# Earlier request of the block inverses and another queue for late stores, in an RWKV-7 attention fused with a squared-ReLU feed-forward

## The chip, the cores and the metric

One core of a Trainium2 chip runs the whole program. The metric is the device time of one execution in microseconds (us). Four executions of the kernel before took 956.38, 958.85, 961.85 and 968.67 us, a median of 960.35 us. The execution that was profiled took 956.67 us, of which the profile's span covers 954.7 us; the rest, 1.97 us, lies around the span.

## What is computed

For each of 4 batches and 8 heads, a 40 x 40 state is carried over 768 time steps, with `y_t = r_t S`, and then `S <- S * w_t - (S a_t) b_t^T + v_t k_t^T`:

```python
for t in range(S):
    y[:, :, t] = np.einsum('bhd,bhde->bhe', rt, state)
    Sa = np.einsum('bhde,bhe->bhd', state, at)
    state_decay = state * wt[:, :, None, :] - np.einsum('bhd,bhe->bhde', Sa, bt)
    state = state_decay + np.einsum('bhd,bhe->bhde', vt, kt)
...
h = np.maximum(x @ w_in, 0.0)          # x: 3072 tokens x 320, w_in: 320 x 2048
return (h * h @ w_out).astype(np.float32)
```

All is float32, the two weights of the second part are float64 in memory.

## The kernel before

**Chunks.** The sequence is cut into 24 chunks of 128 steps (6 along time, 4 batches; chunk i is batch i % 4). Within a chunk the recurrence is solved as a triangular system. For chunk i, `early(i)` (line 360) transposes w, a and b, forms the running products of the decays on VectorE, and multiplies out the triangular matrix N, which ScalarE copies out of PSUM with six copies (lines 398 to 402). N is then stored to DRAM: for chunks from 14 on (`SMALL`), four transfers into `kept_d` and one into `kept_n`. The decays go to `kept_e`.

**Inverses.** GpSimd inverts N's blocks. Chunks are taken in units: chunks 2 to 13 in pairs, then 14 to 17, 18 to 21, and 22 and 23. `take` (line 442) loads a unit's blocks from `kept_q` or `kept_d` into `half_n`, `solving` (line 456) runs the substitution with two tensor operations a step, and stores the result to `kept_t`. For a chunk below 14 only 32 x 32 blocks are inverted, and `inverses(i)` (line 495) puts the 64 x 64 inverse T together. It is a generator of four stages, one taken at each `join()`: (1) request the transfers `blocks` (two, line 508), `N` (line 489) and `spares` (two, line 493); (2) VectorE transposes `blocks` (line 515), ScalarE spreads them into T (line 517); (3) TensorE multiplies (line 525), ScalarE copies (527); (4) TensorE multiplies again (532), ScalarE copies the rest of T (534). `blocks` has one buffer. For a chunk from 14 on, stage 1 loads T as a whole (line 502) and nothing else is left to do.

**Slots.** The first 7 chunks are laid out by hand in a list of steps. Then, for i from 7 to 23, `sorted_slot(i)` (line 973) is one round of some 31 to 38 us: the chain of chunk i (`ch`), everything that chunk j = i + 1 needs (`turn_rv`, `make_rv`, `turn_k`, `turn_down`, `scale_kb`, `make_a`, its `join`s), `early` of one or two chunks ahead (`one`, `two`), and a share of the feed-forward (`thirds`, `whole`, `square`, `make_quarter`). Slot 7 prepares chunks 14 and 15, slot 8 chunks 16 and 17, slots 9 to 14 one chunk each, 18 to 23. Every engine runs its instructions in the order in which this text issues them. `store` and `later` put a transfer off by one or two steps.

**Where the joins stand.** `early_join` is true where chunk j is the second of its pair: stage 1 was then already requested at the end of the slot before, in `loads` (line 956). Where j is the first of a pair (below 14: j = 10 in slot 9 and j = 12 in slot 11) stage 1 comes at line 999, after the slot's fifth step, stage 2 at 1006, stage 3 at 1011 and stage 4 at the end of the slot.

**Queues.** Nearly all transfers are issued by SyncE (SP). Each transfer that SyncE or ScalarE issues takes the next of eight completion semaphores, shared by the two, in turn, and the built program makes it wait until the transfer that had this semaphore before has landed. An engine that issues a transfer stands still during such a wait.

**Buffers that matter here.** `ps_c` and `ps_f` are PSUM pools of two banks each. `turn_state` puts a transposed state into a `ps_c` bank that ScalarE empties into `sd` (line 595); the next chain's first product (`x_`, line 633) needs that bank. `whole` fills both `ps_f` banks, which ScalarE empties into `hid` (line 757).

Of the kernel before, what the change touches and what calls it, by code (L numbers as in the profile page):

```python
# [17 lines left out]
def kernel(  # L18
# [22 lines left out]
    nc = tc.nc  # L41
# [6 lines left out]
    HC = C // 2  # L48
# [11 lines left out]
    at = 0  # L60
    for h, d, n in ((6, 0, D), (7, 0, D), (5, HALF, D - HALF)):
        while n:
# [5 lines left out]
            d, n = d + m_, n - m_  # L68
# [23 lines left out]
    def new(name, shape, bufs):  # L92
        return work.tile(shape, FP32, tag=name, name=name, bufs=bufs)
# [7 lines left out]
    def tick():  # L101
        for entry in line:
            entry[0] -= 1
        while line and line[0][0] <= 0:
            line.pop(0)[1]()
# [3 lines left out]
    def store(out_, in_, steps=2, queue=nc.sync):  # L109
        later(lambda: queue.dma_start(out=out_, in_=in_), steps)  # L110
# [198 lines left out]
    kept_n = [dram.tile([HC, H, HC], FP32, tag=f"n{i}", name=f"kept_n{i}") for i in range(len(order))]  # L309
    Q = HC // 2  # L310
# [17 lines left out]
    def turn(x_):  # L328
        p_ = psum(ps_w)
        for q in range(NP):  # L330
            nc.tensor.transpose(p_[:, q * 128:(q + 1) * 128], pair(x_, q), ident)  # L331
        return quads(p_)

    def products(l_, r_):

        ps = [quads(psum(ps_w)) for _ in range(2)]
        for q in range(NP):
            for e in range(2):
                rows = slice(e * DP, e * DP + D)
                mm(ps[e][:, q], l_[rows, q, :], r_[rows, q, :], True)  # L340
        return ps
# [18 lines left out]
    def early(i, g=None, apart=False):  # L360

        x_ = early_loaded.pop(i)
        dec = decays.next() if g is None else kept_here[i]
        opened = i in opened_early
        if g is not None:
            g["dec"] = dec
            nc.vector.memset(dec[:, :A_, :, MID:MID + 1], 1.0)
        up, down, aT = (dec[:, n] for n in (UP, DOWN, A_))
        wT = turn(x_["w"])
        yield  # L370
        for q in range(NP):
            nc.vector.tensor_tensor_scan(up[:, q, MID + 1:C + 1], wT[:, q, MID:], ones, 1.0, Alu.mult, Alu.mult)  # L372
            nc.vector.tensor_tensor_scan(down[:, q, MID - 1::-1], wT[:, q, MID - 1::-1], ones, 1.0, Alu.mult, Alu.mult)
        yield
        if not apart:
            bT_, aT_ = turn(x_["b"]), turn(x_["a"])
        nc.vector.reciprocal(up[:, :, 0], down[:, :, 0])
        nc.vector.reciprocal(down[:, :, C], up[:, :, C])
        for q in range(NP):
            nc.vector.tensor_tensor_scan(up[:, q, 1:MID], wT[:, q, :MID - 1], ones[:, 1:], up[:, q, 0:1], Alu.mult, Alu.mult)  # L380
            nc.vector.tensor_tensor_scan(down[:, q, C - 1:MID:-1], wT[:, q, C - 1:MID:-1], ones[:, 1:], down[:, q, C:C + 1], Alu.mult, Alu.mult)  # L381
        yield
        if apart:
            bT_, aT_ = turn(x_["b"]), turn(x_["a"])
            yield
        bT = turned("bT", 1)
        nc.vector.tensor_tensor(bT, bT_, down[:, :, 1:C + 1], Alu.mult)
        nc.vector.tensor_tensor(aT[:, :, :C], aT_, up[:, :, :C], Alu.mult)  # L388
        if opened:
            waiting["e", i] = lambda: on_queue[0].dma_start(out=kept_e[i], in_=dec[:USED])  # L390
        else:
            store(kept_e[i], dec[:USED], 2)
        yield
        bb, c = order[i]
        t_ = new("N", [128, 2, H, HC], 1)
        for e, p_ in enumerate(products(bT, aT[:, :, :C])):
            plain, flip_ = t_[:, :, e:NP:2], t_[:, :, NP + e::2]
            nc.scalar.copy(plain, p_[:, ::2].rearrange("s h (f t) -> s f h t", f=2))  # L398
            for half in range(2):
                own_, other = (slice(n * HC, (n + 1) * HC) for n in (half, 1 - half))  # L400
                nc.scalar.copy(flip_[own_, half], p_[other, 1::2, other])
            nc.scalar.copy(flip_[:HC, 1], p_[:HC, 1::2, HC:])
        moved = []
        joins = lambda half, f=Q: t_[half * HC:half * HC + Q, half, :, f:]
        for half in range(2):
            for n in range(2):
                at = half * HC + n * Q
                if i < SMALL:
                    kept, to = kept_q[i, :, half, n], at + Q
                else:  # L410
                    u = unit_of[i]
                    kept, to = kept_d[u][i - units[u][0], :, half], (half + 1) * HC
                    kept = kept[:, n * Q * HC:n * Q * HC + Q * (to - at)].rearrange("h (s t) -> h s t", s=Q)
                moved.append((kept.rearrange("h s t -> s h t"), t_[at:at + Q, half, :, n * Q:to - half * HC], nc.scalar if g is not None and n else nc.sync))
            if i < SMALL and g is None:
                moved.append((kept_m[i][half], joins(half, 0), nc.sync))
        if g is None:
            moved.append((kept_n[i], t_[:HC, 1], nc.sync))
        if opened:
            waiting["n", i] = lambda: [(queue if queue is nc.scalar else on_queue[0]).dma_start(out=to, in_=in_) for to, in_, queue in moved]  # L420
        else:
            for to, in_, queue in moved:
                store(to, in_, 1, queue)
        if g is not None:
            g["N"] = new("N21", [HC, H, HC], 2)
            nc.scalar.copy(g["N"], t_[:HC, 1])
            g["joins"] = spare("joins", i)
            for half in range(2):
                nc.scalar.copy(g["joins"][half * HC:half * HC + Q], joins(half))
        yield  # L430
# [166 lines left out]
    def begin(i, g):  # L597
        g["x"] = loaded.pop(i)
        g["up"], g["aT"] = g["dec"][:, UP], g["dec"][:, A_, :, :C]
# [206 lines left out]
    def run(gen):  # L806
        for _ in gen:
            tick()
# [13 lines left out]
    def prepare(i, g=None, apart=False, steps=0):  # L822
        gen = early(i, g, apart)
        for _ in range(steps):
            next(gen)
            yield
        if i + 1 < len(order) and i + 1 not in early_loaded:
            load_early(i + 1)
        yield from gen
# [97 lines left out]
    for word in """  # L927
# [5 lines left out]
        at = word[len(kind):]  # L933
# [32 lines left out]
    def step(*what):  # L966
        for w_ in what:
            w_()
        tick()
# [3 lines left out]
    def sorted_slot(i, g, ch):  # L973
        j = i + 1
        more = j < len(order)
        n = ready.setdefault(j, {}) if more else None
        made = [prepare(m_, apart=True) for m_ in ahead.get(i, ())]
        one, two = (made + [iter(()), iter(())])[:2]
        if j in inversions:
            n["joining"] = inversions.pop(j)  # L980
        early_join = more and "joining" in n
        joining = n.pop("joining") if early_join else inverses(j, n) if more else iter(())
        fine = more and unit_of[j] < FINE
        join = on(joining)
        of = lambda fn: (lambda: fn(j, n)) if more else (lambda: None)

        if more and "x" in n:
            n.update(up=n["dec"][:, UP], aT=n["dec"][:, A_, :, :C])
        elif more:
            begin(j, n)  # L990
        step(second.make_quarter)
        step(of(turn_rv), on(one), on(one))
        fetch_next(j + 1, "r")
        step(second.make_quarter)
        step(on(ch), of(decay_state))
        step(of(make_rv), second.thirds)
        step(on(ch), on(one))
        if fine:
            join()
        step(second.whole)  # L1000
        step(on(ch))
        step(on(one), of(turn_k))
        step(on(one), on(ch), of(turn_down))
        step(on(ch), of(scale_kb))
        if fine:
            join()
        step(on(ch), of(make_a), second.thirds, on(one))
        fetch_next(j + 1, "v")
        step(of(turn_state), second.square, second.whole, on(two))
        if not early_join:  # L1010
            join()
        run(ch)
        if more:
            begin_chain(j, n)
        loads(j + 1)
        step(second.square, second.make_quarter, on(two), on(two))
        if i in ahead and len(ahead[i]) > 1:
            step(on(two), on(two))
        step(second.make_quarter, on(two))
        for gen in (one, two, joining):  # L1020
            run(gen)

    for i in range(LAID, len(order)):
        tc.no_sync_barrier()
        g = ready.pop(i)
# [41 lines left out]
```

## Time and profile before

| | |
|---|---|
| profiled execution | 956.67 us, span 954.7 us |
| four executions | 956.38 to 968.67 us, median 960.35 us |
| TensorE, matmuls | 903.6 us busy, 95% of the span |
| VectorE / ScalarE / GpSimd | 452.2 / 286.8 / 530.2 us busy |
| mean granted TensorE clock | 0.971 |
| moved by DMA | 103.36 MB, mean 108 GB/s |
| packets of SyncE's queue (q1) and ScalarE's (q10) | 246869 and 2650 |

The page shares the span out by engine, and its chain of waits follows the work that ended last back from the last instruction. The timeline lists one engine's instructions in order of time, merged where they repeat: start, time, engine and line, operation, out<-in, shapes, and in brackets how long the engine stood idle before and who ended it. In SyncE's rows (SPq) the time is that of issuing, and it holds the time for which the queue could take no more. When a transfer lands is read from the trace's completion events. TensorE had these gaps of more than 0.12 us after 300 us of the span: 0.48 us at 364.85, 0.45 us at 402.08, 3.91 us at 423.90, 0.40 us at 870.06.

### The profile page before, as it was taken

To read this page: it belongs to the slowest core of one execution; us is meant where nothing else is said; L and a number is where in the kernel's file an instruction comes from. 1 tells how busy PE (TensorE), PEld (TensorE's weight loads), DVE (VectorE), ACT (ScalarE), POOL (GpSimd) and SP (SyncE) were. 2 spreads that over 40 slices of the span, in tenths; PEclk is the share of its full clock that TensorE was granted. 3 is DMA by queue.
4 is the path that set the end of the run, shared out by engine and by line. 5 is a ranking of instruction groups with operands and counts; after the bars stand their busy time and mean duration, and the time that the engine had idled before them with its cause. 6 is when DMAs were issued, how large, how long until landed. Compare 5 with 4: busy or idle time off the path is not lost.

```text
span 954.7 us, 22650 instructions
## 1 busy us (share of the span) xinstructions
PE 903.6 (95%) x9156; PEld 717.8 (75%) x9156; DVE 452.2 (47%) x1064; ACT 286.8 (30%) x735; POOL 530.2 (56%) x1001
## 2 busy tenths in 40 slices
PE   5878989779999999989999999999999999999998
PEld 4545656558787887878888888888888878887776
DVE  4526738787863455543654554543334432231110
ACT  3223244444533233323333332222212222222111
POOL 4788518265018678139999849999768850000000
PEclk9989979799999999999999999999999999999999
DMA  9689777785875587994554786605664154120000
GB/s 110 127 153 178 151 138 150 165 184 119 165 134 129 110 174 127 168 177 81 115 91 83 131 171 113 113 19 82 137 110 75 35 108 79 39 35 9 13 14 14
DMA packets 253223, 103.36 MB, mean 108 GB/s; under 512 B 234144, under 2 KB 240160, under 8 KB 251968
## 3 DMA queue, kind: packets, MB, share of 16 engines
q1 hardware_dynamic: 246869, 83.43, 48.5%
q0 software_dynamic: 3600, 16.25, 7.2%
q10 hardware_dynamic: 2650, 2.25, 0.8%
q8 instruction: 72, 1.18, 0.6%
q14 instruction: 32, 0.25, 0.1%
HBM read 69.00 MB, written 30.92 MB: 105 GB/s over the span
## 4 chain that ended last, share of the span: by engine, by line
PE 72%; DVE 4%; DMA 3%; ACT 1%; SPq 1%; issue 1%; ACTq 0%; DVEq 0%
PE ps_f L87 40%; PE ps_w L87 13%; PE ps_c L87 12%; PE ps_w L331 4%; PE ps_c L593 1%; DMA hid<-in_moe_w_out_dram 1%; PE ps_c L666 1%; DMA dec<-kept_e 1%; PE ps_w L577 1%; DMA blocks<-kept_t 1%; SPq L508 1%; DVE decay L381 0%; DVE decay L380 0%; DVE decay L388 0%; DVE hid L764 0%
## 5 line engine op out<-in xcount | busy, mean ns | idle before, releaser
L477 POOL TENSOR_TENSOR half_p<-half_n,half_t 128x126 f32<-128x126 f32 (+44 forms) x437 | 231.9, 531 | 75.6 <-DMA half_n<-kept_d 22.4
L479 POOL TENSOR_TENSOR half_t<-half_t,half_p 128x126 f32<-128x126 f32 (+44 forms) x437 | 248.2, 568 | 34.3
L87 PE MATMUL ps_f<-w_out,hid 128*128 128x320 f32 x768 | 218.7, 436 | 0.0
L87 PEld LDWEIGHTS ps_f<-w_out,hid 128*128 128x128 f32 x768 | 142.0, 190 | 54.0 <-issue 0.2
L87 PE MATMUL ps_f<-tokens,w_in 128*128 128x256 f32 x672 | 157.8, 389 | 0.0
L87 PEld LDWEIGHTS ps_f<-tokens,w_in 128*128 128x128 f32 x672 | 126.9, 194 | 18.7 <-issue 1.7
L764 DVE TENSOR_TENSOR hid<-hid 128x512 f32<-128x512 f32 x96 | 81.0, 882 | 50.1 <-ACT hid L757 49.7
L757 ACT ACTIVATE hid<-ps_f 128x512 f32<-128x512 f32 x84 | 49.9, 597 | 84.1 <-PE ps_f L87 84.1
L264 PE MATMUL ps_f<-ident 128*128 128x512 f32 (+2 forms) x148 | 70.6, 615 | 0.0
L451 POOL DMA_DIRECT2D half_n<-kept_q x18 | 9.4, 528 | 78.0 <-DMA kept_q<-N 31.1
L692 DVE TENSOR_TENSOR tokens<-ps_c,dec 128x512 f32<-128x512 f32 x24 | 16.6, 690 | 76.2 <-PE ps_c L87 76.2
L347 DVE TENSOR_TENSOR RV<-ps_w,upper 128x512 f32<-128x512 f32 x48 | 30.9, 686 | 45.7 <-PE ps_w L87 45.4
L372 DVE TENSOR_TENSOR_SCAN decay<-ps_w,ones 128x64 f32<-128x64 f32 x88 | 23.9, 271 | 60.0 <-PE ps_w L331 59.9
L264 PEld LDWEIGHTS ps_f<-ident 128*128 128x128 f32 x148 | 29.0, 213 | 26.6 <-issue 25.5
L87 PE MATMUL ps_f<-tokens,w_third 64*128 64x256 f32 x336 | 45.5, 380 | 3.3 <-ACT hid L757 3.3
L347 DVE TENSOR_TENSOR RX<-ps_w,upper 128x512 f32<-128x512 f32 x48 | 30.8, 684 | 37.2 <-PE ps_w L87 36.9
L543 DVE TENSOR_TENSOR kvT<-ps_w,dec 128x512 f32<-128x512 f32 x24 | 16.5, 687 | 62.0 <-ACT minus_x L653 35.2
L87 PEld LDWEIGHTS ps_c<-xr,T 64*64 64x64 f32 x768 | 28.0, 139 | 19.6 <-issue 16.3
L398 ACT COPY N<-ps_w 128x256 f32<-128x256 f32 x48 | 17.7, 368 | 80.7 <-PE ps_w L87 54.6
L565 DVE TENSOR_TENSOR f<-end,dec 128x4 f32<-128x4 f32 x20 | 5.4, 271 | 67.9 <-DMA dec<-kept_e 67.9
L555 ACT COPY rT<-ps_w 128x512 f32<-128x512 f32 x24 | 14.0, 584 | 77.6 <-PE ps_w L331 77.5
L87 PE MATMUL ps_w<-decay,bT 40*128 40x128 f32 x352 | 28.2, 294 | 7.7 <-DVE RX L347 3.9
(146 smaller groups left out, 1432.7 us busy)
## 6 DMA issues: line engine op xcount, KB each, us to landing
dec<-kept_e SPq DMA_DIRECT2D x22, 633.8 KB
kept_e<-decay SPq DMA_DIRECT2D x19, 633.8 KB
in_w<-in_w_dram SPq DMA_DIRECT2D x24, 160.0 KB
in_b<-in_b_dram SPq DMA_DIRECT2D x24, 160.0 KB
in_ab<-in_a_dram SPq DMA_DIRECT2D x24, 160.0 KB
in_r<-in_r_dram SPq DMA_DIRECT2D x24, 160.0 KB
in_v<-in_v_dram SPq DMA_DIRECT2D x24, 160.0 KB
out_dram<-o SPq DMA_DIRECT2D x24, 160.0 KB
```

The costliest lines, as they stand in the source:

```text
L87: nc.tensor.matmul(o, l_, r_, start=start, stop=True, skip_group_check=True)
L264: nc.tensor.matmul(fill_bank[:, :n * 128], ident, ident.unsqueeze(1).to_broadcast([128, n, 128]), start=True, stop=True, skip_group_check= ...
L331: nc.tensor.transpose(p_[:, q * 128:(q + 1) * 128], pair(x_, q), ident)
L347: nc.vector.tensor_tensor(t_, p_, over4(upper), Alu.mult)
L372: nc.vector.tensor_tensor_scan(up[:, q, MID + 1:C + 1], wT[:, q, MID:], ones, 1.0, Alu.mult, Alu.mult)
L398: nc.scalar.copy(plain, p_[:, ::2].rearrange("s h (f t) -> s f h t", f=2))
L477: nc.gpsimd.tensor_tensor(p_, part[:, at:at + m_].unsqueeze(1).to_broadcast([128, n, m_]), t3[:, :n, s:s + 1].to_broadcast([128, n, m_]), ...
L479: nc.gpsimd.tensor_tensor(t3[:, :n, s + 1:], t3[:, :n, s + 1:], p_, Alu.subtract)
L543: nc.vector.tensor_tensor(kT, kT_, down[:, :, 1:C + 1], Alu.mult)
L692: nc.vector.tensor_tensor(t_, y_, g["up"][:, :, :C], Alu.mult)
L757: nc.scalar.activation(h_, p_.rearrange("p f t -> p (f t)"), Act.Relu)
L764: nc.vector.tensor_tensor(h_, h_, h_, Alu.mult)
```

## The change

Two edits. Stores of N (`kept_d` and `kept_n`) of chunks that are not in the hand-laid opening, that is from 14 on, are issued by ScalarE instead of SyncE: five transfers for each of ten chunks. And stage 1 of `inverses` for the first chunk of a pair is taken right after the slot's first `make_quarter` instead of at line 999, so that each of its later stages moves one join ahead (stage 2 to line 999, stage 3 to 1006); the join at line 1011 is left out for these slots.

```diff
@@ early
-                moved.append((kept..., t_[...], nc.scalar if g is not None and n else nc.sync))
+                moved.append((kept..., t_[...], nc.scalar if not opened or g is not None and n else nc.sync))
...
-            moved.append((kept_n[i], t_[:HC, 1], nc.sync))
+            moved.append((kept_n[i], t_[:HC, 1], nc.sync if opened else nc.scalar))
@@ sorted_slot
         step(second.make_quarter)
+        if fine and not early_join:
+            join()
         step(of(turn_rv), on(one), on(one))
...
         step(of(turn_state), second.square, second.whole, on(two))
-        if not early_join:
+        if not early_join and not fine:
             join()
```

In the built program SyncE issues 50 transfers fewer and ScalarE 50 more. In slots 9 and 11 `blocks`, `N` and `spares` stand on SyncE's queue ahead of the loads of w, b, a and r and of the output's store, where they stood behind them; on VectorE the transpose of `blocks` stands before `kvT`, where it stood after the scaling of k and b; on TensorE stage 3 stands before the products for RX. On ScalarE the five stores stand right behind N's six copies. In slots 7 to 14 what follows them is `sd` and two `hid`; for the second chunk that slots 7 and 8 prepare (15 and 17) it is T's last copies (line 534), `rT` and `kvT`.

## The prediction

> **What bounds the kernel now.** I read the page first: what bounds, and what share is not matmuls.
>
> ```profile
> PE 903.6 (95%) x9156; PEld 717.8 (75%) x9156; DVE 452.2 (47%) x1064; ACT 286.8 (30%) x735; POOL 530.2 (56%) x1001
> PE 72%; DVE 4%; DMA 3%; ACT 1%; SPq 1%; issue 1%; ACTq 0%; DVEq 0%
> ```
>
> TensorE bounds it; only what makes TensorE wait can change the time. Then the chain of waits in order of time, where the slots begin to repeat (start, us, what):
>
> ```profile
> 413.27 3.67 PE ps_f L87 x16
> 417.90 3.89 SPq L508
> 421.84 4.80 DMA blocks<-kept_t
> 427.81 2.67 PE ps_w L87 x16
> 431.53 4.14 PE ps_f L87 x16
> ```
>
> In slot 9 the end hangs on SyncE's issue of `blocks` and its landing at 426.64; TensorE restarts at 427.81. It is the one long gap after 300 us (3.91 us). The table by stretches, slot 9 against slot 10:
>
> ```profile
> core 0: us, PE busy (x) PEld busy (x) DVE busy (x) ACT busy (x) POOL busy (x), PEclk, DMA share, GB/s
> 402.50:440.50 38.00, 34.06 (x412) 29.24 (x412) 15.24 (x39) 13.52 (x38) 17.98 (x31) 0.91 0.76 138
> 440.50:474.80 34.30, 34.30 (x417) 28.78 (x413) 17.74 (x42) 11.54 (x31) 31.95 (x31) 1.00 0.57 105
> ```
>
> Slot 9 lost matmul time and clock (0.91 against 1.00); slot 10, whose `blocks` were requested a slot earlier, lost neither. Last, the timelines of ScalarE, TensorE and SyncE where slot 8 begins, since there the moved stores get a new place:
>
> ```profile
> 368.60 0.26 ACT L402 COPY N<-ps_w 64x128 f32<-64x128 f32 x1
> 368.76 0.74 ACT L534 COPY T<-ps_w 32x256 f32<-32x256 f32 x2
> 369.94 0.58 ACT L555 COPY rT<-ps_w 128x512 f32<-128x512 f32 x1 [0.44 <-PE ps_w L331]
> 370.43 0.59 ACT L556 COPY kvT<-ps_w 128x512 f32<-128x512 f32 x1
> ```
>
> ```profile
> 372.87 0.66 PE L87 MATMUL ps_c<-xr,T 64*64 64x40 f32 x16
> 373.46 1.16 PE L87 MATMUL ps_w<-rT,kvT 40*128 40x128 f32 x16
> ```
>
> ```profile
> 366.95 0.45 SPq L960 DMA_DIRECT2D dec<-kept_e  x1
> 367.50 0.39 SPq L146 DMA_DIRECT2D in_k<-in_k_dram  x1
> 368.61 4.63 SPq L508 DMA_DIRECT2D blocks<-kept_t  x2
> ...
> 468.30 1.82 SPq L110 DMA_DIRECT2D kept_d<-N  x4
> 470.21 0.50 SPq L110 DMA_DIRECT2D kept_n<-N  x1
> ```
>
> T's last copy stands right behind N's copies of chunk 15, with 3.4 us to spare before TensorE needs T, and `kvT` with 2.4 us. Five stores take 2.41 us to issue from an empty queue (468.30 to 470.71).
>
> **The early request, slot 9.** From the first product after `sd` to the first w_out matmul of the quarter, TensorE takes 440.52 - 420.67 = 19.85 us in slot 9 and 474.79 - 462.07 = 12.72 us in slot 10, with the same matmuls: 7.1 us to win (3.91 gap, some 2.8 from the halved clock, 426.0 to 432.8 in the trace's clock records, the rest order). Is it all won? `blocks` must have landed when VectorE ends its scans at 415.3; up to `kvT` at 419.08 lateness would still be free. In the new order SyncE gets to `blocks` behind `kept_e` of chunk 17. The last users of the one `blocks` buffer are the stage-4 matmuls ending at 404.3, and 17's N stores (405.52 to 409.43) no longer stand between. So it is issued at about 405 to 408, and lands at 410 to 411, behind the 634 KB of `kept_e` (409.27). What could spoil it is GpSimd's load of the next unit, two transfers of 768 KB issued at 410.88; whatever SyncE issued just then landed only at 423.9 to 426.2. The request is ahead of it by some 3 to 5 us.
>
> **Slot 11.** The same stretch takes 509.36 - 496.34 = 13.02 us, without a wait for `blocks`: 0.3 us to win. Together -7.4 us.
>
> **What the five transfers are moved past.** w, b, a and r, and the output's store, go some 3.9 us later on SyncE (486.74 to 490.66 for the same five in slot 11). r landed at 424.5 and is turned at 447.9; w, b and a serve the slot after; the output's store frees a buffer used once a slot. Cost zero; without that cover it would be the 3.9 us.
>
> **The stores, in mid-slot (eight chunks: 14, 16, 18 to 23).** Behind them on ScalarE wait `sd` and two `hid`. In slot 10 N's copies end at 468.84 and `sd` at 469.33. With 2.41 us of issuing `sd` ends at about 471.8; the `x_` products that need its bank start at 473.19, so 1.3 us stay (1.3 to 1.7 in the slots where I read it). The second `hid` ends at 473.0, the quarter that needs its bank starts at 474.79. Cost zero, if five issues take under 3.7 us. Bounds: 2.1 us from ScalarE's own rows (two `kept_q` in 0.82), 4.97 us from SyncE's row with a full queue (376.75 to 381.72). I take 2.4, since ScalarE's queue carries 2650 packets and SyncE's 246869. At 4.97 each slot loses 1.2 us. Their semaphore waits are for loads that landed well before, but for slot 13, where `kept_e` and v stand behind GpSimd's 768 KB: I allow 0.3 us (0 to 1).
>
> **The stores at a slot's end (15 and 17).** Here the built program gives ScalarE's third store of chunk 15 a wait for `in_k`, and the fifth a wait for the second `blocks` transfer. Before, these landed at 373.98 and 375.31, behind `dec` issued at 366.95, while N's copies end at 368.86. Taking 14's stores off SyncE starts the eight `tokens` copies when VectorE's `tokens` is done (357.8) instead of at 360.2. From their start to `dec` an unhindered slot takes 6.3 us (438.95 to 445.27): `dec` is issued at 364.2. From `dec` to the second landing three slots took 8.36, 8.86 and 9.30 us: 372.5 to 373.5. Then comes the fifth issue, 0.5, T's copies, 0.74, `rT` and `kvT`, 1.1: `kvT` ends at 374.9 to 375.9 and its product starts at 375.0 to 376.0 instead of 373.46. Cost 1.6 to 2.6, I take 2.1. If SyncE gains nothing, `kvT` ends at 377.6 and the cost is 4.3.
>
> Does this gap also halve the clock? The rows have 3.91 us that did and 0.48 us that did not, so its price lies between 0 and 2.8 us; two pieces of about 1.5 and 0.6 us are nearer to the small row, and I take 0. The Trainium skill, TensorE: Matmul & The Clock Gate, Part 1, says that the clock falls after an idle window of about 3.4 us; the 3.91 us agree, and no row here shows a gap of 2 us. By that rule the sum below stands; by the long row it would be -2.0.
>
> Chunk 17's waits are met (its fifth is for a `dec` that lands by 405.5, its copies end at 406.06). The issues alone push T's copies to end at 409.4, needed at 410.06, and `kvT` to 410.4, needed at 410.65. I take 0.2 (0 to 1).
>
> **What SyncE gains by the stores** is the 2.4 us used above, and no more: 50 issues leave it, but none stands on the chain elsewhere. The Trainium skill, DMA: Bandwidth & Descriptors, Issuing engines are not separate DMA queues, speaks against more: all queues share the same 16 DMA engines, so moving only saves issue time. A gain beyond it is not in the sum.
>
> **Sum.** -7.4 + 2.1 + 0.2 + 0.3 = -4.8 us: 956.67 becomes 951.9 for an execution like the profiled one. That one lies 3.7 us under the median of four; a median should come to 960.35 - 4.8 = 955.6 us.
>
> **Rivals.**
> (a) ScalarE pays more, and it ends slower. The place is ScalarE's queue behind N's copies. If five issues take 4.97 us, eight mid-slots lose 1.2 each, 9.6, and slot 8's start 4.3 with a clock drop of 2.8: +16.7 - 7.4 = +9.3, some 970 us. With 2.6 us already lost, it decides from 0.6 us a mid-slot on, that is from about 4.3 us for five issues. For it: issues on SyncE do reach 1.8 us each. Against it: only on the queue that is full.
> (b) `blocks` stay late in slot 9, since the 768 KB loads come first: landing near 424, VectorE then stands before `kvT` and more waits behind it. No gain, 2 to 3 us lost: 960 to 963 us. Against it: 3 to 5 us of lead.
> (c) ScalarE's waits cost nothing, because `blocks` land sooner than I think: -7.4, 953 us.
> (d) The early request does nothing. Excluded for slot 9 as long as that stall recurs in other executions; one trace can't say.
>
> **Chances.** Forecast (gain of 3 to 7) 0.58; (a), from break-even up to its full price, 0.18; (b) or (d) 0.10; (c) and better 0.14. Executions of one kernel spread over 12 us, so 1% (9.6 us) is about what can be told from no change. Over 1% faster needs nearly twice my sum: 0.10, a part of (c) with a lucky median. Over 1% slower needs all of (a): 0.07. The range goes from (c) with 4 us of scatter, 949, to (b) and half of (a), 964.
>
> **What would show it.** Right: in slot 9 no gap before the products for bT, a clock of 1.00, 12.7 us for the stretch; `blocks` landed before 415. At slot 8's start five stores behind N's copies with the last held some 2 to 4 us, T's copies at 373 to 374, a TensorE gap of 1 to 2 us. In mid-slots `sd` later by 2.4 us and no gap. Wrong: gaps before the `x_` products, two long gaps, or a gap moved to the start of slots 9 or 10.

## The result and the profile after

The changed kernel takes 958.39 us (median of 54 executions, 952.65 to 965.15) against 961.68 us for the kernel before (78 executions, 954.71 to 968.67). The ratio is 0.9969, with a 95% interval of 0.9958 to 0.998: a gain of 0.3%, some 3 us, where the forecast was 4.8 us (0.5%). A second timing of the same program, 12 executions beside 24 of the kernel before, gave 0.9946 with an interval of 0.9921 to 0.997; the two intervals overlap. The profiled execution took 953.79 us, span 952.1 us.

The page after, with the lines for busy time, two queues and the chain of waits:

```profile
PE 904.7 (95%) x9156; PEld 719.0 (76%) x9156; DVE 451.2 (47%) x1064; ACT 286.6 (30%) x735; POOL 529.3 (56%) x1001
q1 hardware_dynamic: 235189, 80.15, 47.1%
q10 hardware_dynamic: 14330, 5.53, 2.5%
PE 74%; DMA 3%; SPq 1%; ACT 1%; DVE 1%; issue 0%; ACTq 0%; DVEq 0%
```

The stores have moved: 11,680 packets left SyncE's queue (q1) and came to ScalarE's (q10). VectorE's share of the chain fell from 4% to 1%. The table by stretches, slot 9 and slot 10:

```profile
406.80:437.80 31.00, 30.95 (x413) 26.87 (x413) 14.71 (x40) 13.11 (x38) 12.22 (x23) 1.00 0.78 159
437.80:472.00 34.20, 34.20 (x414) 28.73 (x412) 17.76 (x40) 11.55 (x31) 31.69 (x33) 1.00 0.60 104
```

The first numbers of a row are the stretch, its length and TensorE's busy time; the granted clock comes third from the end. Slot 9 took 38.0 us before and takes 31.0 us now, with a clock of 1.00 instead of 0.91. SyncE in that slot:

```profile
408.67 1.79 SPq L508 DMA_DIRECT2D blocks<-kept_t  x2
411.58 0.49 SPq L489 DMA_DIRECT2D N<-kept_n  x1
412.39 1.24 SPq L493 DMA_DIRECT2D spares<-kept_m  x2
```

`blocks` landed at 412.12 and 412.54, `spares` at 415.26 and 415.42; GpSimd issued its 768 KB at 415.08 and 415.60. The early request is ahead of them, as forecast.

What was given back stands at the start of slot 8. ScalarE and TensorE there:

```profile
370.08 0.31 ACTq L110 DMA_DIRECT2D kept_d<-N  x1
370.35 0.26 ACT L402 COPY N<-ps_w 64x128 f32<-64x128 f32 x1
370.43 4.62 ACTq L110 DMA_DIRECT2D kept_d<-N  x3
375.38 0.45 ACTq L110 DMA_DIRECT2D kept_n<-N  x1
375.88 0.75 ACT L534 COPY T<-ps_w 32x256 f32<-32x256 f32 x2 [5.27 <-DMA kept_d<-N]
376.65 0.59 ACT L555 COPY rT<-ps_w 128x512 f32<-128x512 f32 x1
377.13 0.59 ACT L556 COPY kvT<-ps_w 128x512 f32<-128x512 f32 x1
```

```profile
376.29 1.04 PE L87 MATMUL ps_c<-xr,T 64*64 64x40 f32 x16 [1.57 <-ACT T L534]
377.78 1.16 PE L87 MATMUL ps_w<-rT,kvT 40*128 40x128 f32 x16 [0.44 <-ACT kvT L556]
```

The third store of chunk 15 is held until `in_k` has landed (373.78), the fifth until the second `blocks` has (375.31). T's copies, `rT` and `kvT` wait behind them, and TensorE loses 1.57 and 0.44 us. In this execution the granted clock stays at 1.0 there, and from 223 us of the span to its end.

To add such pieces up, I line up one group of products that every trace has, the transposes of r at the start of each slot, and take how much later than in the first profile of the kernel before they start. The difference of two such shifts is what the stretch between them cost. In the profile after it is +2.5 us over slot 8's start, -7.1 us over slot 9, +0.1 us from there on: -4.4 us, close to the forecast's -4.8 us. The time over all executions fell by less. So either this execution was a lucky one, or the traces of before and after differ in the opening; the experiments decide.

### The profile page after: what moved, and what is told of

Read it like the earlier page. It is cut to its first block, busy times and chain, and to the rows that moved or that the text cites. A ratio compares the mean times of both kernels' runs of the same rounds, so it can differ in the third digit from the quotient of the medians.

```text
span 952.1 us, 22620 instructions
## 1 busy us (share of the span) xinstructions
PE 904.7 (95%) x9156; PEld 719.0 (76%) x9156; DVE 451.2 (47%) x1064; ACT 286.6 (30%) x735; POOL 529.3 (56%) x1001
## 4 chain that ended last, share of the span: by engine, by line
PE 74%; DMA 3%; SPq 1%; ACT 1%; DVE 1%; issue 0%; ACTq 0%; DVEq 0%
PE ps_f L87 40%; PE ps_w L87 14%; PE ps_c L87 12%; PE ps_w L331 4%; PE ps_c L593 1%; PE ps_c L666 1%; DMA dec<-kept_e 1%; PE ps_w L577 1%; DMA in_k<-in_k_dram 1%; SPq L705 1%; DMA spares<-kept_m 0%; DMA hid<-in_moe_w_out_dram 0%; DMA tokens<-tokens 0%; SPq L146 0%; DMA blocks<-kept_t 0%
## 5 line engine op out<-in xcount | busy, mean ns | idle before, releaser
L87 PE MATMUL ps_c<-xr,T 64*64 64x40 f32 x768 | 34.4, 234 | 3.0 <-ACT T L534 2.1
L87 PEld LDWEIGHTS ps_f<-tokens,w_third 64*128 64x128 f32 x336 | 30.4, 187 | 7.6 <-ACT hid L757 5.0
```

The costliest lines, as they stand in the source:

```text
L87: nc.tensor.matmul(o, l_, r_, start=start, stop=True, skip_group_check=True)
```

## The experiments

One table for all profiles, in us, worked out as above and rounded last (negative is a gain):

| profile | slot 8's start | slot 9 | after slot 9 | sum from slot 7 | ratio of times, 95% interval |
|---|---|---|---|---|---|
| the change, 1st | 2.5 | -7.1 | 0.1 | -4.4 | 0.9969 [0.9958, 0.998] |
| the change, 2nd (after_again) | 7.1 | -6.7 | 0.1 | 0.6 | 0.9946 [0.9921, 0.997] |
| the change, 3rd (after_third) | 1.8 | -7.1 | 0.1 | -5.1 | |
| the change, 4th (after_fourth) | 3.5 | -7.1 | 0.1 | -3.4 | |
| the change, 5th (after_fifth) | 1.6 | -7.0 | 0.1 | -5.3 | |
| early_alone | 0.1 | -4.1 | -0.3 | -4.3 | 0.9953 [0.9925, 0.9982] |
| stores_alone | 4.9 | -6.5 | 0.5 | -1.1 | 0.9974 [0.9948, 1.0] |
| fifteen_sync | 0.0 | -7.0 | 0.2 | -6.8 | 0.9945 [0.992, 0.997] |
| sync_again | 0.0 | -6.7 | 0.1 | -6.5 | 0.9924 [0.9894, 0.9954] |
| fifth_sync | 1.1 | -6.7 | 0.1 | -5.5 | 0.9929 [0.9899, 0.996] |
| request_back | 0.0 | -6.2 | 0.4 | -5.8 | 0.9924 [0.9893, 0.9956] |
| fifteen_late | 9.9 | -7.0 | 0.1 | 3.1 | 0.9999 [0.9974, 1.0025] |
| the kernel before, 2nd (before_again) | 0.0 | 0.4 | 0.0 | 0.4 | |

**The early request alone** (all stores back on SyncE):

```diff
-... nc.scalar if not opened or g is not None and n else nc.sync))
+... nc.scalar if g is not None and n else nc.sync))
...
-            moved.append((kept_n[i], t_[:HC, 1], nc.sync if opened else nc.scalar))
+            moved.append((kept_n[i], t_[:HC, 1], nc.sync))
```

> The early request alone; all stores of N stay on SyncE. If slot 9's wait for blocks is worth 7.1 us in every execution, and the request still gets ahead of GpSimd's two transfers of 768 KB, it is 7.0 to 7.4 us faster than before (ratio 0.9925) and TensorE's long gap in slot 9 is gone. If it needs the stores of chunk 17 out of its way on SyncE, blocks land near 424 and VectorE stands before kvT: between 0 and 3 us slower (1.000 to 1.003). If the halved clock that follows slot 9's gap comes only in a part of the executions, the gain is 4.3 to 7.1 us and the ratio lies between 0.9926 and 0.9955.

957.1 us, ratio 0.9953, which lies in the expectation's third case, but not for its reason. Slot 8's start costs nothing, so that price belongs to the stores. Slot 9 gives 4.1 us, not 7. Its gap and the stretch of 3.4 us around it, TensorE's timeline and the table by stretches:

```profile
423.67 0.94 PE L87 MATMUL ps_w<-spares 32*32 32x32 f32 x32 [1.04 <-DVE in_b L583]
```

```profile
422.70:426.10 3.40, 2.39 (x58) 2.27 (x60) 1.32 (x4) 0.73 (x2) 2.29 (x7) 1.00 1.50 142
```

The releaser named, VectorE's `in_b`, is not the last: the first `spares` transfer, issued at 413.14 behind GpSimd's first 768 KB (412.77), landed at 423.53, 0.14 us before the products of `spares` start. With 17's stores of N still on SyncE, the request comes too late for its last two transfers. And this gap of 1.04 us is followed by a clock of 0.5 from 426.1 on, for 3.4 us.

**The stores alone** (the request back where it was):

```diff
-        if fine and not early_join:
-            join()
...
-        if not early_join and not fine:
+        if not early_join:
             join()
```

> The stores on ScalarE alone; blocks are requested where they were. If the cost at slot 8's start is a fixed 2.5 us as in the trace of the changed kernel, and slot 9's wait stays, the ratio is 1.0026. If the gap at slot 8's start halves the clock in a part of the executions, the cost is 2.5 to 5.3 us, 1.003 to 1.0055. If taking the stores off SyncE lets blocks be issued sooner in slot 9 by itself, slot 9's gap shrinks and the ratio is below 1.

961.34 us, ratio 0.9974. Two things here are not in the forecast. Slot 9's stall is gone without the early request (-6.5 us). And slot 8's start costs 4.9 us though its gaps are only 0.73 and 0.44 us: the granted clock is halved right behind them. The table by stretches:

```profile
376.00:379.40 3.40, 2.17 (x34) 1.92 (x36) 0.48 (x3) 2.59 (x7) 2.90 (x7) 1.00 0.94 199
379.40:382.80 3.40, 3.40 (x26) 2.46 (x23) 3.40 (x13) 0.80 (x3) 2.88 (x7) 0.50 0.75 154
382.80:386.20 3.40, 3.40 (x9) 2.70 (x8) 0.36 (x2) 1.11 (x3) 2.77 (x9) 0.50 0.89 147
```

After a stretch in which TensorE was busy 2.17 of 3.40 us, two stretches have a clock of 0.50 (26 and 9 matmuls), though TensorE is busy all through both.

**Chunk 15's stores back on SyncE**, the rest as changed:

```diff
-... nc.scalar if not opened or g is not None ...
+... nc.scalar if not opened and i != 15 or g is not None ...
...
-            moved.append((kept_n[i], t_[:HC, 1], nc.sync if opened else nc.scalar))
+            moved.append((kept_n[i], t_[:HC, 1], nc.sync if opened or i == 15 else nc.scalar))
```

> The changed kernel, but chunk 15's five stores go back to SyncE; the other nine chunks' stay on ScalarE. If the shortfall is chunk 15's stores holding ScalarE at slot 8's start, TensorE has no gap of over 0.5 us there, and the ratio to the kernel before falls from 0.9969 by 2.5 us or more, to 0.9945 or less (0.9925 if slot 9's stall is worth 7.1 us in every execution). If the stores of the other chunks cost time that the one trace did not show, it stays near 0.997.

955.14 us, ratio 0.9945. Taking five of the 50 stores back removes all of slot 8's price and keeps slot 9's gain.

**The kernel before, once more:**

> The kernel before, unchanged, for a second profile. If slot 9's gap halves the clock in every execution, its stretch from the first product after sd to the first w_out matmul takes 19.9 us again. If that depends on where the clock's windows fall, it takes between 17.1 and 19.9 us.

961.01 us, span 959.0 us. Slot 9 has a gap of 4.02 us at 427.82 and a halved clock from 430.5 on for 6.8 us: within 0.4 us the stall is the same. The start of slot 7 is 3.9 us later than in the first profile, from the opening, which the change doesn't touch.

**The change, four more executions.** No edit; the first was timed as well.

> The change once more, unaltered, beside the three runs that vary chunk 15's stores. Theory: slot 8's start makes TensorE wait in pieces of 0.4 to 1.6 us and these halve the clock in some executions only; so the stretch of slot 8's start costs 2.5 us here (as in the first profile of the changed kernel) or about 5 (as where the stores were moved alone), and slot 9 gives about 7.0 back; time about 958.5 us, some 3 us over the version that leaves chunk 15's stores on SyncE. Rival, the forecast as it stands: the clock is not touched by pieces this short, the cost is 2 to 2.6 us in every execution, and the time is 2 us over that version, 957.2 us.

> One more execution of the change, unaltered, for its trace alone. Theory: slot 8's start costs 2.5 us, or about 5 where the clock is halved behind its gaps; with the other profiles of the same instructions there this gives a first count of how often. Rival, the forecast: 2 to 2.6 us with a clock of 1.0.

> The change once more, for its trace. Four profiles with these instructions at slot 8's start cost 2.5, 4.9, 7.1 and 1.8 us, the second and third with a halved clock. Theory: the records' clock changes only on a grid of 3.413 us, and it is halved after a stretch of the grid that holds 1.0 us of gap or more together with products on a quarter of the array; so the cost is 1.8 to 2.6 us where the grid cuts the wait for T and the wait for kvT apart so that neither stretch holds that much, and 4.9 to 7.1 us where one stretch holds it. Rival, the forecast: a gap this short never halves the clock, and 2 of 4 was chance from another source; then clock and grid show no such relation.

> The same as the run before it, one more execution: 1.8 to 2.6 us with a clock of 1.0, or 4.9 to 7.1 us with a halved clock behind a stretch of the grid with 1.0 us of gap or more. All six then average 3 to 5 us by the theory, 2.1 by the forecast.

958.0, 955.99, 958.12 and 956.53 us (the first a median of 12, the rest one execution each). With the first profile, five executions of the same instructions pay 2.5, 7.1, 1.8, 3.5 and 1.6 us at slot 8's start, 3.3 on average. The 2nd and the 4th have a halved clock there. The 2nd, TensorE's timeline and the table by stretches:

```profile
380.01 1.04 PE L87 MATMUL ps_c<-xr,T 64*64 64x40 f32 x16 [1.53 <-ACT T L534]
381.50 2.08 PE L87 MATMUL ps_w<-rT,kvT 40*128 40x128 f32 x16 [0.44 <-ACT kvT L556]
```

```profile
377.60:381.00 3.40, 1.79 (x20) 1.02 (x18) 1.30 (x5) 1.35 (x4) 2.85 (x7) 0.99 1.02 203
381.00:384.40 3.40, 2.96 (x23) 2.73 (x24) 0.79 (x2) 1.23 (x4) 2.85 (x7) 0.50 0.85 193
384.40:387.80 3.40, 3.40 (x26) 2.40 (x23) 2.98 (x12) 1.38 (x4) 2.85 (x8) 0.50 0.58 107
```

The gaps are 1.53 and 0.44 us, no longer than in the first profile (1.57 and 0.44), but the products for `kvT` take 2.08 us instead of 1.16, and the clock records show 0.5 from 381.0 on for 10.2 us, three stretches of which two are shown. The expectation had about 5 us for this case; it was 7.1, and 3.5 in the 4th, where one stretch is halved: the expected sizes were too narrow, on both sides.

That clock and grid are related was expected of the last two before they ran. In the 4th, gaps of 0.93 us and 0.44 us fall into one stretch of the grid (377.3 to 380.7, TensorE busy 1.95 us of it), and half clock follows. In the 5th, 0.69 and 0.44 us are cut by a border at 380.3 (busy 2.38 and 3.21 us), and the clock stays. But the first of these two stretches holds 1.0 us without work as well, so the expectation's limit, 1.0 us of gap, doesn't tell the two cases apart; the last section has what does.

**Chunk 15's stores behind what they held up:**

```diff
             for to, in_, queue in moved:
-                store(to, in_, 1, queue)
+                store(to, in_, 4 if i == 15 else 1, queue)
```

> The change, but chunk 15's five stores are issued by ScalarE behind T's copies, rT and kvT instead of ahead of them. Theory: what costs at slot 8's start is only that T's copies, rT and kvT stand behind held stores; with them ahead no gap above 0.6 us is left there and no halved clock, the stretch costs 0 to 0.3 us, slot 9 gives 7 back, and the time is that of the version with chunk 15's stores on SyncE, 955.1 us, ratio 0.993 to 0.996. Rival: the held stores then stand before o and minus_x of slot 8, TensorE waits a little later, and the time is that of the change, 958 us, ratio 0.997.

963.31 us, ratio 0.9999: the theory missed, the rival was right, and its price was far higher than it said. ScalarE's timeline, then TensorE's:

```profile
379.62 5.67 ACTq L110 DMA_DIRECT2D kept_d<-N  x4
...
386.40 0.43 ACT L785 COPY o<-ps_f 128x320 f32<-128x320 f32 x1 [8.93 <-DMA kept_d<-N]
```

```profile
386.88 2.07 PE L87 MATMUL ps_f<-tokens,w_third 64*128 64x256 f32 x6 [5.38 <-ACT o L785]
```

T, `rT` and `kvT` are on time, but four steps later SyncE has already taken the semaphores for `kept_e` (634 KB) and the loads of the next chunk. The fourth store is issued at 384.91, when `kept_e` has landed (384.89), the fifth at 385.91, behind w (385.83). Now o waits on ScalarE, and TensorE for o's bank: a gap of 5.38 us, with a clock of 0.5 for 10.2 us from 384.7 on. So the order on ScalarE alone doesn't make such a store free; what holds it is the landing of the transfer eight places before it.

**Only the fifth store on SyncE** (four stay on ScalarE):

```diff
-            moved.append((kept_n[i], t_[:HC, 1], nc.sync if opened else nc.scalar))
+            moved.append((kept_n[i], t_[:HC, 1], nc.sync if opened or i == 15 else nc.scalar))
```

> The change, but of chunk 15's five stores the last one (kept_n, which in the changed kernel is held until the second blocks transfer has landed) is issued by SyncE, behind the stores of kept_e. The other four stay on ScalarE, the third held until in_k has landed. Theory: the cost of slot 8's start is the hold and follows its length; without the last hold T's copies start some 1.0 to 1.2 us earlier, at most 0.6 us of gap is left before T's product, no one stretch of 3.4 us loses more than 1 us and the clock stays at 1.0, so slot 8's start costs 0.6 to 1.5 us and slot 9 gives 7.0: about 1 us over the version with all five on SyncE, ratio 0.993 to 0.996. Rival: the price comes from ScalarE's issuing as such and from in_k; then the cost stays at 2 to 5 us, ratio 0.996 to 0.998.

953.26 us, ratio 0.9929. ScalarE's timeline:

```profile
377.11 0.75 ACT L534 COPY T<-ps_w 32x256 f32<-32x256 f32 x2 [3.80 <-DMA kept_d<-N]
```

T's copies stood idle 3.80 us instead of 5.27 (and 4.4 to 5.3 in the other executions of the change), TensorE has one gap of 0.44 us, the clock stays at 1.0, and slot 8's start costs 1.1 us, as expected. The price follows the length of the hold, with five stores on ScalarE as with four. Where the clock stays at 1.0, slot 8's start costs 1.1, 1.6, 1.8 and 2.5 us with T's copies held up for 3.80, 4.39, 4.56 and 5.27 us: each time the hold less 2.7 to 2.8 us. Chunk 17's stores fit too. In the 2nd execution of the change T's copies are held up for 3.12 us at slot 9's start, and TensorE waits there:

```profile
423.68 1.16 PE L87 MATMUL ps_w<-rT,kvT 40*128 40x128 f32 x16 [0.30 <-ACT kvT L556]
```

**All five on SyncE, beside it** (the same edit as fifteen_sync):

> The version with all five stores of chunk 15 on SyncE, again, beside the one with only the last of them there. Theory: no gap over 0.6 us after 300 us, clock 1.0, a net gain of 6 to 7 us after slot 7, ratio 0.991 to 0.996, and 0 to 2 us below the other version. Rival: the first profile of it was a lucky one, and its own slot 8 or 9 shows a gap here; ratio 0.997.

952.77 us, ratio 0.9924. No gap over 0.41 us after 300 us, a clock of 1.0 from 261 us on, -6.5 us from slot 7.

**The stores but for chunk 15's, without the early request:**

```diff
-... nc.scalar if not opened or g is not None ...
+... nc.scalar if not opened and i != 15 or g is not None ...
...
-        if fine and not early_join:
-            join()
...
-        if not early_join and not fine:
+        if not early_join:
             join()
```

(`kept_n` of chunk 15 as in fifteen_sync.)

> Stores of N on ScalarE but for chunk 15, and the request for blocks where it was before. Theory: relieving SyncE is enough by itself for slot 9; the blocks are issued ahead of GpSimd's 768 KB and slot 9 gives 6.5 us, slot 8's start costs nothing, and the time is within 1 us of the version with both (955.1 us), ratio 0.993 to 0.997. Rival, the forecast's own: it is the early request that wins slot 9; without it, and with chunk 15's stores still on SyncE, the blocks come behind the 768 KB again, a gap of some 4 us stands in slot 9, and the time is that of the kernel before, 961 to 962 us.

956.47 us, ratio 0.9924. Slot 9's stall is gone here too, and TensorE has no gap over 0.44 us there. How close it is, SyncE's and VectorE's timelines show:

```profile
414.14 1.33 SPq L508 DMA_DIRECT2D blocks<-kept_t  x2
```

```profile
424.77 0.45 DVE L515 STREAM_TRANSPOSE spares<-blocks 128x256 f32<-128x256 f32 x1 [0.27 <-DMA blocks<-kept_t]
```

GpSimd's first transfer of 768 KB was issued at 414.04, 0.1 us ahead of `blocks`, which landed at 421.16 and 424.68. VectorE waited 0.27 us for it, TensorE not at all. In the kernel before SyncE reached `blocks` at 417.90, after 5.23 us in which it stood in the issue of the output's store (412.58 to 417.81). Relieved of the stores it issues the output's store at 413.69 in 0.36 us, ahead of GpSimd's transfers. Whether moving that one store would do by itself wasn't tried.

## Why the prediction was right in its mechanism and wrong in its size

**The step that failed: "Does this gap also halve the clock? ... I take 0."** That term of the sum, 0, measured 5.1 and 1.5 us in two of five executions, 1.3 us on average. The forecast bounded the price of the halving at slot 8's start between 0 and 2.8 us and took the low end, because two pieces of about 1.5 and 0.6 us seemed nearer to the row that did not halve it. The pieces came out as forecast in the first profile (1.57 and 0.44 us), but the clock is halved behind them in two of five executions of the change, and behind 0.73 and 0.44 us in the run with the stores alone. Without a halving slot 8's start cost 2.5, 1.8 and 1.6 us, 2.0 on average: the term of 2.1 us itself was right. (The forecast's own start times, 375.0 to 376.0 instead of 373.46, make 1.5 to 2.5 us, not 1.6 to 2.6.) With it, 7.1 and 3.5 us, and 4.9 us in stores_alone; so one halving cost more than the 2.8 us that were the upper bound. The average of five, 3.3 us, is 1.2 us over the term.

Executions without a trace point the same way. The time at half clock of an execution is 2 x (1 - mean granted clock) x span. It averages 68.5 us in the kernel before (64 executions, standard error 0.9), 65.0 us in the change (54, 1.1; the 12 of the second timing average 67.4) and 61.8 us with chunk 15's stores on SyncE (17, 1.4). Between the first and the last lie the 6.8 us of slot 9's halved clock; the change gives some 3 us of them back (3.2, standard error 1.8). Two halved executions in five, with 10.2 and 3.4 us, make 2.7 us.

**The sum with measured terms.** Averages of the five profiles: -6.97 us (slot 9), +3.31 us (slot 8's start), +0.14 us (all that follows, slot 11's gain included) make -3.5 us by the traces; the medians differ by 961.68 - 958.39 = 3.3 us. The forecast's range and its sign were right; its gain was too large by that one term. The time itself, 958.39 us where 955.6 was forecast, is off by 2.8 us: 1.5 us by the gain, and 1.3 us because the median of four executions that it started from, 960.35 us, lay that far below the median of 78.

**What was right.** Slot 9's gain: 7.1 us forecast, 6.7 to 7.1 measured. Slot 11: 0.3 us forecast, 0.2 measured. Stores in mid-slot at no cost: in slot 10 N's stores take 465.59 to 467.96, `sd` follows at 468.01, and TensorE has no gap. Instead of 0.3 us in slot 13 there is 0.1 us in each of slots 10, 12, 13 and 14, in all versions with the stores on ScalarE and not in early_alone; where on the path it lies was not followed. Chunk 17, 0.2 us forecast (0 to 1): 0.4 us in the 2nd execution, by the gap of 0.30 us shown above, and nothing in the other four; it is why slot 9 gave 6.7 us there and 7.0 to 7.1 in the others. The five transfers put behind the request cost nothing.

**Right in size, wrong in its cause.** The forecast gave slot 9's gain to the early request and wrote that SyncE's relief is "the 2.4 us used above, and no more". The relief alone gives 6.5 us in slot 9 (6.2 in request_back), the early request alone 4.1; together 7. The two cover the same stall: SyncE's queue has to reach `blocks`, or `spares`, before GpSimd's 768 KB or just behind. The working contained this (17's stores of N "no longer stand between") but not that it was enough. The Trainium skill, DMA: Bandwidth & Descriptors, Issuing engines are not separate DMA queues, says that initiating on several engines saves only the time to initiate. That is still what happened, but 5 us of standing on the issuing engine is not small where a load stands behind it.

**Rivals.** (a) had the right place, ScalarE behind N's copies, and a clock drop at slot 8's start, and its price for that start, 4.3 + 2.8 = 7.1 us, was reached in one execution of five; but it put most of its price on mid-slots, which cost next to nothing. (b) did not occur. (c) is refuted by the hold itself, and stands only when chunk 15's stores go back to SyncE. (d) is refuted for slot 9: the stall is there in both profiles of the kernel before.

**A better version.** With chunk 15's stores on SyncE the ratios are 0.9945 and 0.9924, a gain of 0.55 and 0.76%. fifth_sync and request_back lie at 0.9929 and 0.9924; the intervals of all of these overlap, so which of the three is best stays open, and by times alone the interval of after_again (0.9921 to 0.997) overlaps them as well. It is the traces that separate them.

## What to carry to other kernels

A transfer that is moved to an engine which also computes brings its wait along: ask which landing it is held by and what stands behind it on that engine, in the worst slot and not the typical one; here 45 of 50 moved stores cost next to nothing and five gave back almost half of the gain. Price a short gap on TensorE with a chance of half clock behind it, not as all or nothing, look at how much work the products around it hold, and take several traces before a gap's price is believed. And when two edits come with different reasons, run each alone: here each removes most of the same stall.

## What the runs showed of the hardware

**The clock is decided on a fixed grid, and a stretch of it needn't be empty.** In every trace, the borders between clock records lie 3.413 us or a multiple of it apart, whatever the work. The Trainium skill, TensorE: Matmul & The Clock Gate, Part 1, describes such a free-running window of 3413 ns, and these records agree. But its rule for the fall, an idle window of about 3.4 us, which the forecast named, did not hold: TensorE was busy for 1.79, 1.95, 2.17 and 2.39 of 3.4 us in stretches that half clock followed. Even the 3.91 us gap of the kernel before, which the forecast took to agree with it, is cut by a border, and the stretch that the fall at 426.0 followed held work:

```profile
422.60:426.00 3.40, 1.30 (x15) 0.89 (x12) 0.00 (x0) 0.00 (x0) 1.90 (x6) 0.99 1.01 163
```

The clock stayed full after stretches with 2.38 (5th execution of the change), 2.58 and 2.7 us, and in the first profile after one with only 2.13:

```profile
372.60:376.00 3.40, 2.13 (x8) 1.14 (x7) 2.69 (x11) 0.12 (x1) 2.85 (x8) 1.00 1.12 167
376.00:379.40 3.40, 2.58 (x38) 2.30 (x40) 0.43 (x1) 2.47 (x7) 2.85 (x8) 1.00 0.97 221
```

There the border at 376.0 cut the gap in two, and the busy part before it was w_out's products on the full 128 x 128 array, where the halved stretch with 2.39 us held mostly products on 32 x 32 or 40 x 128.

The 14 traces together show what orders these cases better. For each stretch of the grid at full clock I add up the work of its products, that is rows times columns of the array used times width (a product cut by a border counts in proportion to its time). After 300 us, leaving out the program's end, the seven stretches that half clock followed hold 1.0 to 20.5 million multiplications, those just named with 1.79, 1.95, 2.17 and 2.39 us busy 19.6, 17.3, 15.0 and 17.5; none of the others holds less than 23.7, and the one with 2.13 us holds 39.9. Over all 3557 stretches, the opening included, of which half clock followed 114, one limit of 23.2 million misplaces 5. The best limit on busy time misplaces 26: half clock followed up to 3.02 us busy and did not follow as little as 1.51. The densest stretches hold 67 million. The limit was found in these same traces, and no run varied the array's use by itself; but by it, a gap among small products is dearer than the same gap among full ones.

**The same instructions cost 1.6 to 7.1 us** at one place, as the hold is longer or shorter and the border of the grid falls in one place or another. The opening adds its own scatter: at the start of slot 7, with nothing changed before it, the profiles lie 1.8 to 6.5 us behind the first one of the kernel before, which was thus the earliest of all and a poor one to measure a median from.
